# The short form of h - tanh(h) alone, with a test of its range and a general path behind it

## The chip, the cores and the metric

The kernel runs on one core of a Trainium2 chip. The metric is the device time of one execution in microseconds (us), as the median of several runs. TensorE is PE in the profile (its weight loads are PEld), VectorE is DVE, ScalarE is ACT, GpSimd is POOL, and SyncE, which issues every DMA of this kernel, is SP.

## What is computed

Three layers follow one another. An attention in which 32 packed queries p of each head first gather keys and values, and the 576 queries of a sequence then attend to the 32 packed rows; a layer with the odd nonlinearity h - tanh(h); and a layer in which each token goes to one of eight experts. Cut to what matters:

```python
p_packed = sm_attn(p, k, v)                      # 8 batches, 8 heads, 32 packed rows of 64
out = sm_attn(q, p_packed, p_packed)             # 8 batches, 8 heads, 576 rows of 64
x = out.transpose(0, 2, 1, 3).reshape(4608, 512)
h = x @ w_in                                     # w_in 512 x 2048
x = (h - np.tanh(h)) @ w_out                     # w_out 2048 x 512
logits = x @ w_gate + modality_bias[modality_id] # 8 experts, one per token by argmax
out[mask] = gate_w[mask, None] * (np.maximum(x[mask] @ w1[e], 0.0) @ w2[e])
```

The weights of the middle layer come as 64-bit floats. Matrix products are done in fp32, or, where a stage is long, as three products of rounded parts (hi by hi, lo by hi, hi by lo).

## The kernel before

Since the second attention is a product with p_packed, its output need not be formed: h of a head is a2 (the softmax of 32 columns) times M = p_packed times w_in. The kernel forms M per batch (m_pe, eight products of 512 columns, lines 195 to 235, `at<-ws,ppT` and `mh`, `ml` in the profile) and the attention weights a2 per half batch of 288 tokens (sm2a to sm2d, lines 454 to 498).

The work is cut into slots. In the first part, 256 slots: 16 half batches, each with 16 blocks f of 128 columns of w_in. A slot n does gemm1 (`h<-a,m`, a block of 128 x 288 of h), then chain(n), which makes g = h - tanh(h) out of it, then gsplit, which makes two rounded parts `gh` and `gl`, and three slots later gemm2 (`acc<-gh,wo_hi` and so on), which adds g times a block of w_out into four accumulators. The first 32 slots (half batches 0 and 1) use plain fp32 in gemm1, and the first 16 in gemm2. Between them stand the conversion of the 64-bit weights (conv_a, 32 chunks, lines 159 to 178, on DVE, ACT and POOL), the attention of the next batch, its M, and the logits of half batches that are done. In the second part, 144 slots, the one expert that token 0 goes to is applied to all tokens (gemm1b, relu, gemm2b). At the end the kernel reads a flag of whether any token goes to another expert, and if so does those in other_experts.

chain(n), lines 731 to 752, holds eight instructions, each over 128 x 288 elements. On ACT: u = h squared (L741), th = tanh(h) (L742), mk = a scaled square of h as an integer, which is zero where h squared is under the threshold U_THR = 0.0775 (L743), qq = exp(-PK u) (L744). On DVE: th = h - th (L745), qq = (qq + PB) u (L747), gs = PA qq h (L749), and a predicated copy (L751), which puts th into gs where mk is not zero. So gs holds a short form of h - tanh(h), PA h u (exp(-PK u) + PB), where h is small, and the difference elsewhere. The tiles u, qq, th and mk have one buffer each. The products h stand in two PSUM buffers (ps_h); one comes free when the last instruction of chain that reads it is done. gsplit (lines 754 to 763) rounds gs to gh on ACT (L760) and takes gl = gs - gh (L762) on DVE or, from slot 16 on for seven of sixteen slots, on POOL:

```python
eng = nc.gpsimd if n >= 16 and n % 16 in [3, 5, 7, 9, 11, 13, 15] else nc.vector
eng.tensor_tensor(out=gl, in0=gs, in1=f32(gh), op=ALU.subtract)
```

A scheduling layer sets the final order of each engine's instructions out of the order in which the program is written, its dependencies and its own durations. Each engine then runs its list in that order.

Of the kernel before, what the change touches and what calls it, by code (L numbers as in the profile page):

```python
# [26 lines left out]
def attn_moe_moe_kernel(  # L27
# [131 lines left out]
    def conv_a(key):  # L159
        raw = raws[key].rearrange("p a c -> p (a c)")  # L160
        hi, lo = raw[:, 1::2], raw[:, 0::2]
        nc.vector.tensor_scalar(
            out=lo, in0=lo, scalar1=29, scalar2=0x40000000, op0=ALU.logical_shift_right, op1=ALU.bitwise_or
        )
        yield
        nc.vector.scalar_tensor_tensor(
            out=lo, in0=hi, scalar=3, in1=lo, op0=ALU.logical_shift_left, op1=ALU.bitwise_xor
        )
        yield
        nc.scalar.activation(out=hi, in_=hi.bitcast(F32), func=ACTF.Copy, scale=16384.0)  # L170
        nc.scalar.activation(out=hi.bitcast(F32), in_=hi, func=ACTF.Sign)
        nc.scalar.activation(out=lo.bitcast(F32), in_=lo.bitcast(F32), func=ACTF.Abs)
        v = hi.bitcast(F32)
        if key[0] == 0:
            v = early.tile([128, 512], F32, name="wv", tag="wv", bufs=6)
        elif key[1] < NWH // 2:
# [70 lines left out]
    def attention(ap, b, ps_of):  # L247
# [177 lines left out]
        def ppt_ev():  # L425
            ps = ps_of("ppt", 0)
            t = ppT[b] = ap.tile([128, 4, 32], F32, name="ppT", tag="ppT", bufs=2)
            nc.scalar.activation(out=t.rearrange("p h j -> p (h j)"), in_=ps[:, 0, 128:256], func=ACTF.Copy)

        def scores2(half):  # L430
            ps = ps_of("s2", half)
# [44 lines left out]
        def sm2c(half):  # L476
# [134 lines left out]
    def flags_a():  # L611
# [8 lines left out]
            yield  # L620
        fl["has"] = has

    def flags_pe():
# [5 lines left out]
    def flags_b():  # L629
        other = evp.tile([1, NE], F32, name="other", tag="rt_m")  # L630
        nc.vector.tensor_tensor(
            out=other, in0=em8[0:1, :], in1=idx_t[0:1, 0:1].to_broadcast([1, NE]), op=ALU.not_equal
        )
        n = evp.tile([1, NE, NHB], F32, name="n_other", tag="rt_l")
        nc.vector.tensor_tensor(
            out=n, in0=fl["ps"].rearrange("o (e h) -> o e h", e=NE),
            in1=other.unsqueeze(2).to_broadcast([1, NE, NHB]), op=ALU.mult,
        )
# [4 lines left out]
        yield  # L643
        nc.vector.tensor_copy(out=flags[:, 0:NE, 0:NHB], in_=n)
        nc.vector.tensor_copy(out=flags[:, :, NHB], in_=tot)
        yield


    def other_experts():
        gd, idd = (nc.dram_tensor(nm, [NBLK, 32], F32, kind="Internal").ap() for nm in ("gate_d", "idx_d"))  # L650
        hi_f = 32
        n_any = nc.values_load(flags[0:1, NE, NHB:NHB + 1], min_val=0, max_val=hi_f)
# [200 lines left out]
    def relu(n):  # L853
        ps = ht.pop(n)
        if n % 2:
            gh, gl = (
                gp.tile([128, TB], F32R, name="bg", tag=tg) for tg in (("u", "qq") if n % 4 == 1 else ("th", "mk"))
            )
        else:
            gh = g3.tile([128, TB], F32R, name="bh", tag="gh")  # L860
# [44 lines left out]
    def seq(fns):  # L905
        for fn in fns:
            res = fn()
            if isgenerator(res):
                yield from res
            else:  # L910
                yield


    with ExitStack():
# [79 lines left out]
        for f in range(NWH // 2):  # L994
            at_cv(NWH + 1 + f * 11 // 7, lambda f=f: conv_b((1, f)))


        def run(*fns):
            for _ in seq(fns):
                pass  # L1000
# [173 lines left out]
```

## Time and profile before

| what | value |
|---|---|
| median of 3 runs | 1284.15 us (1283.78 to 1285.51) |
| the profiled execution's own time | 1284.04 us |
| its span, first to last instruction | 1282.3 us |
| PE busy | 1210.1 us, 94% |
| DVE busy | 838.4 us, 65% |
| ACT busy | 710.3 us, 55% |
| POOL busy | 166.3 us, 13% |
| mean granted TensorE clock | 0.983 |

By the starts of u, slot 0 begins at 41.0 us, slot 16 at 114.5, slot 32 at 186.1, slot 208 at 721.2, and the second part at 864.3 us; the last matmul ends at 1271.5 us. A share of the whole span is a mean over stages with different limits, so the rows further down are cut at these times. A row of busy time reads: the stretch, its length, then for PE, PEld, DVE, ACT and POOL the busy time and the count of instructions, the granted clock, the DMA engines' busy share and GB/s. What is missing in PE's busy time to the length of a stretch is time in which PE had nothing to do.

### The profile page before, as it was taken

What the parts mean: (1) busy time and instruction counts of PE and PEld (TensorE: products, weight loads), DVE (VectorE), ACT (ScalarE), POOL (GpSimd) and SP (SyncE); (2) the same over time, 40 slices, a digit from 0 to 9 for tenths busy, and PEclk for the clock granted to TensorE, in tenths of its full rate; (3) what the DMA queues carried; (4) which work ended last, traced back from release to release, by engine and by line L of the source; (5) the groups of instructions that cost most, each with busy time, mean ns of one, the idle gap of its engine ahead of it and who ended that gap; (6) DMA issues with size and microseconds to landing.
All of it is one profiled execution on the core that took longest, in us unless ns stands there. A gap on an engine that the chain in (4) does not pass through costs nothing.

```text
span 1282.3 us, 25934 instructions
## 1 busy us (share of the span) xinstructions
PE 1210.1 (94%) x9762; PEld 1049.7 (82%) x9763; DVE 838.4 (65%) x1941; ACT 710.3 (55%) x1832; POOL 166.3 (13%) x174
## 2 busy tenths in 40 slices
PE   5688889999999999999999999999999999999996
PEld 2455668889889889979979978989899999999995
DVE  4987999898998898998898897884111111111111
ACT  3888867678678678678677777772111111111111
POOL 1322211121111111111111122240000000000000
PEclk7799899999999999999999999999999999999998
DMA  8766344454354344344345126212122222222201
GB/s 241 213 201 197 104 131 118 106 131 121 73 129 119 73 125 124 73 118 128 73 108 139 39 83 194 79 51 74 63 83 67 82 61 76 64 65 83 66 17 35
DMA packets 189843, 132.36 MB, mean 103 GB/s; under 512 B 122640, under 2 KB 167696, under 8 KB 189712
## 3 DMA queue, kind: packets, MB, share of 16 engines
q1 hardware_dynamic: 189712, 130.65, 36.6%
q8 instruction: 78, 1.28, 0.4%
q14 instruction: 53, 0.43, 0.1%
HBM read 98.10 MB, written 32.51 MB: 102 GB/s over the span
## 4 chain that ended last, share of the span: by engine, by line
PE 68%; DVE 16%; issue 7%; ACT 4%; DMA 3%; POOL 2%; SPq 0%; POOLq 0%; DVEq 0%; ACTq 0%
PE acc L98 12%; PE acc L100 12%; PE acc L99 11%; PE h L98 9%; PE h L99 8%; PE h L100 8%; PE at L202 2%; DVE gs L749 2%; DVE th L745 2%; DVE gs L751 2%; DVE gl L762 1%; PE at L340 1%; DVE qq L747 1%; DMA w1s<-in_moe_w_dram 1%; DVE s L466 1%
## 5 line engine op out<-in xcount | busy, mean ns | idle before, releaser
L98 PE MATMUL acc<-gh,wo_hi 128*128 128x288 f32 x960 | 293.9, 308 | 6.4 <-ACT gh L760 4.0
L100 PE MATMUL acc<-gl,wo_hi 128*128 128x288 f32 x960 | 277.0, 298 | 5.4 <-DVE gl L762 2.9
L99 PE MATMUL acc<-gh,wo_lo 128*128 128x288 f32 x960 | 281.9, 295 | 0.0
L98 PEld LDWEIGHTS acc<-gh,wo_hi 128*128 128x128 f32 x960 | 180.4, 188 | 42.2 <-ACT u L741 13.2
L100 PEld LDWEIGHTS acc<-gl,wo_hi 128*128 128x128 f32 x960 | 177.6, 188 | 13.5 <-DVE gl L762 6.2
L99 PEld LDWEIGHTS acc<-gh,wo_lo 128*128 128x128 f32 x960 | 180.6, 188 | 0.4 <-issue 0.2
L100 PE MATMUL h<-xbl,w1h 128*128 128x256 f32 x576 | 162.3, 282 | 0.0
L99 PE MATMUL h<-xbh,w1l 128*128 128x256 f32 x576 | 162.1, 281 | 0.0
L98 PE MATMUL h<-xbh,w1h 128*128 128x256 f32 x576 | 161.5, 280 | 0.0
L762 POOL TENSOR_TENSOR gl<-gs,gh 128x288 fp32r<-128x288 f32 x105 | 85.7, 817 | 569.4 <-ACT gh L760 398.4
L745 DVE TENSOR_TENSOR th<-h,th 128x288 f32<-128x288 f32 x256 | 114.8, 449 | 53.8 <-ACT mk L743 51.2
L751 DVE COPY_PREDICATED gs<-mk,th 128x288 f32<-128x288 int32 x256 | 140.1, 547 | 2.6
L98 PE MATMUL h<-ah,mh 128*128 128x288 f32 x448 | 135.2, 302 | 6.5 <-DVE gs L749 6.5
L741 ACT ACTIVATE u<-h 128x288 f32<-128x288 f32 x256 | 106.0, 414 | 63.3 <-PE h L100 40.8
L863 DVE SCALAR_TENSOR_TENSOR bl<-h,bh 128x256 fp32r<-128x256 f32 x72 | 30.6, 425 | 164.0 <-ACT bh L862 163.9
L99 PE MATMUL h<-ah,ml 128*128 128x288 f32 x448 | 132.2, 295 | 0.0
L100 PE MATMUL h<-al,mh 128*128 128x288 f32 x448 | 131.8, 294 | 0.0
L747 DVE SCALAR_TENSOR_TENSOR qq<-qq,u 128x288 f32<-128x288 f32 x256 | 122.7, 479 | 12.8 <-ACT qq L744 9.9
L744 ACT ACTIVATE qq<-u 128x288 f32<-128x288 f32 x256 | 114.6, 448 | 27.1 <-DVE gs L749 21.9
L760 ACT ACTIVATE gh<-gs 128x288 fp32r<-128x288 f32 x240 | 107.6, 449 | 35.3 <-PE acc L99 33.8
L742 ACT ACTIVATE th<-h 128x288 f32<-128x288 f32 x256 | 104.6, 409 | 34.9 <-DVE gs L751 32.2
L862 ACT ACTIVATE bh<-h 128x256 fp32r<-128x256 f32 x72 | 27.6, 384 | 171.3 <-PE h L100 169.8
(163 smaller groups left out, 2426.4 us busy)
## 6 DMA issues: line engine op xcount, KB each, us to landing
ws<-w_in_v SPq DMA_DIRECT2D x56, 512.0 KB
nat<-in_v_dram SPq DMA_DIRECT2D x16, 576.0 KB
x_hi<-x2h SPq DMA_DIRECT2D x16, 576.0 KB
x_lo<-x2l SPq DMA_DIRECT2D x16, 576.0 KB
xbh<-x_hi SPq DMA_DIRECT2D x18, 512.0 KB
xbl<-x_lo SPq DMA_DIRECT2D x18, 512.0 KB
raw<-in_moe_w_in_dram SPq DMA_DIRECT2D x32, 256.0 KB
raw<-in_moe_w_out_dram SPq DMA_DIRECT2D x16, 512.0 KB
```

Of the source, the lines that this page charges most:

```text
L98: nc.tensor.matmul(out=ps, lhsT=ah, rhs=bh, start=first, stop=False)
L99: nc.tensor.matmul(out=ps, lhsT=al, rhs=bh, start=False, stop=False)
L100: nc.tensor.matmul(out=ps, lhsT=ah, rhs=bl, start=False, stop=last)
L741: nc.scalar.activation(out=u, in_=ps, func=ACTF.Square)
L742: nc.scalar.activation(out=th, in_=ps, func=ACTF.Tanh)
L744: nc.scalar.activation(out=qq, in_=u, func=ACTF.Exp, scale=-PK)
L745: nc.vector.tensor_tensor(out=th, in0=ps, in1=th, op=ALU.subtract)
L747: nc.vector.scalar_tensor_tensor(out=qq, in0=qq, scalar=PB, in1=u, op0=ALU.add, op1=ALU.mult)
L751: nc.vector.copy_predicated(gs, mk, th)
L760: nc.scalar.activation(out=gh, in_=gs, func=ACTF.Copy)
L762: eng.tensor_tensor(out=gl, in0=gs, in1=f32(gh), op=ALU.subtract)
L863: nc.vector.scalar_tensor_tensor(out=gl, in0=ps, scalar=0.0, in1=f32(gh), op0=ALU.max, op1=ALU.subtract)
```

## The change

In chain, tanh, the mask, the difference and the predicated copy are gone, so two instructions are left on ACT and two on DVE; u and qq have two buffers each. Every gl is now taken by DVE. The threshold is tested ahead of time instead: the entries of a head's a2 row add up to one, so the absolute h is at most the sum over eight heads of the largest absolute entry of M. After each product of M a new DVE instruction (m_bound) takes the largest absolute entry of each partition, 64 in all; near the end flags_a compares the largest of them with 0.998 sqrt(U_THR) / 8 and the count of partitions above it is added to the flag that the kernel reads at its end. If it is not zero, a new function redo computes the first two layers again with tanh, from a2, p_packed and w_in, which therefore are written to DRAM: a2 of each half batch (16 DMAs) and p_packed of each batch (8 DMAs), on SP's queue.

```diff
+    ones_b = const.tile([128, 1], F32, name="ones_b")
+    m_max = const.tile([128, B, NU], F32, name="m_max")
...
     def m_ev(b, u, ps=AT):
...
             mt[b, u] = (t,)
+            m_bound(b, u, t)
             return
...
         nc.vector.tensor_tensor(out=lo, in0=ps, in1=f32(hi), op=ALU.subtract)
-        yield
+        m_bound(b, u, f32(hi))
+        yield
+
+    def m_bound(b, u, t):
+        nc.vector.tensor_reduce(
+            out=m_max[:, b, u:u + 1], in_=t.rearrange("p g c -> p (g c)"), axis=AX.X, op=ALU.max,
+            apply_absolute_value=True,
+        )
...
+            nc.sync.dma_start(out=pp_d[b], in_=t)
...
+            nc.sync.dma_start(out=a2_d[2 * b + half], in_=t.rearrange("p g c -> p (g c)"))
...
+        nc.vector.tensor_reduce(out=t, in_=m_max.rearrange("p b u -> p (b u)"), axis=AX.X, op=ALU.max)
+        nc.vector.tensor_scalar(out=t, in0=t, scalar1=0.998 * U_THR ** 0.5 / H, scalar2=None, op0=ALU.is_gt)
...
+        nc.tensor.matmul(out=AT[0:1, 1, 0:1], lhsT=ones_b, rhs=fl["big"], start=True, stop=True)
...
         with tc.If(n_any > 0):
+            n_big = nc.values_load(flags[0:1, NE, 0:1], min_val=0, max_val=128)
+            with tc.If(n_big > 0):
+                redo()
...
     def chain(n):
         ps = ht.pop(n)
-        u = gp.tile([128, HW], F32, name="u")
-        qq = gp.tile([128, HW], F32, name="qq")
-        th = gp.tile([128, HW], F32, name="th")
-        mk = gp.tile([128, HW], I32, name="mk")
+        u = gp.tile([128, HW], F32, name="u", bufs=2)
+        qq = gp.tile([128, HW], F32, name="qq", bufs=2)
...
         nc.scalar.activation(out=u, in_=ps, func=ACTF.Square)
-        nc.scalar.activation(out=th, in_=ps, func=ACTF.Tanh)
-        nc.scalar.activation(out=mk, in_=ps, func=ACTF.Square, scale=(0.5 / U_THR) ** 0.5)
         nc.scalar.activation(out=qq, in_=u, func=ACTF.Exp, scale=-PK)
-        nc.vector.tensor_tensor(out=th, in0=ps, in1=th, op=ALU.subtract)
         yield
         nc.vector.scalar_tensor_tensor(out=qq, in0=qq, scalar=PB, in1=u, op0=ALU.add, op1=ALU.mult)
         yield
         nc.vector.scalar_tensor_tensor(out=gs, in0=qq, scalar=PA, in1=ps, op0=ALU.mult, op1=ALU.mult)
-        yield
-        nc.vector.copy_predicated(gs, mk, th)
...
-        eng = nc.gpsimd if n >= 16 and n % 16 in [3, 5, 7, 9, 11, 13, 15] else nc.vector
-        eng.tensor_tensor(out=gl, in0=gs, in1=f32(gh), op=ALU.subtract)
+        nc.vector.tensor_tensor(out=gl, in0=gs, in1=f32(gh), op=ALU.subtract)
```

DVE's list between the softmax of batch 4 and that of batch 5, before (th, qq, gs, gl and mk are the tiles of chain and gsplit; ml is the low part of M; what an instruction waits for stands in brackets):

```order
L747 SCALAR_TENSOR_TENSOR qq<-qq,u 128x288 [waits Activation_49]
L745 TENSOR_TENSOR th<-h,th 128x288 [waits DVE_49,Activation_49]
L749 SCALAR_TENSOR_TENSOR gs<-qq,h 128x288 [waits DVE_49,Pool_49]
L762 TENSOR_TENSOR gl<-gs,gh 128x288 [waits PE_49,Activation_49]
L751 COPY_PREDICATED gs<-mk,th 128x288 [waits DVE_49]
L747 SCALAR_TENSOR_TENSOR qq<-qq,u 128x288 [waits Activation_49]
L745 TENSOR_TENSOR th<-h,th 128x288 [waits DVE_49,Activation_49]
L749 SCALAR_TENSOR_TENSOR gs<-qq,h 128x288 [waits DVE_49]
L751 COPY_PREDICATED gs<-mk,th 128x288 [waits DVE_49]
```

And the same engine between the same two softmaxes now:

```order
L872 TENSOR_TENSOR gl<-gs,gh 128x288 [waits PE_49,Activation_49]
L860 SCALAR_TENSOR_TENSOR qq<-qq,u 128x288 [waits Activation_49]
L862 SCALAR_TENSOR_TENSOR gs<-qq,h 128x288 [waits DVE_49]
L872 TENSOR_TENSOR gl<-gs,gh 128x288 [waits PE_49,Activation_49]
L860 SCALAR_TENSOR_TENSOR qq<-qq,u 128x288 [waits Activation_49]
L862 SCALAR_TENSOR_TENSOR gs<-qq,h 128x288 [waits DVE_49]
```

Two slots took eight instructions of chain and one gl; they now take four and two gl, and each gl, which waits for PE and ACT, stands in front of the next slot's qq and gs.

DVE's list at the start of the program, before (s is the softmax of half batch 0 or 1, m its sums, a2w its finished weights, which the first gemm1 reads; raw is a chunk of 64-bit weights):

```order
L483 RECIPROCAL m_356<-m_356 128x18 [waits DVE_49]
L466 TENSOR_TENSOR s_375<-s_375,m_378 128x576
L485 TENSOR_TENSOR s_330<-s_330,m_356 128x576 [waits DVE_49]
L162 TENSOR_SCALAR raw_345<-raw_345 128x512 [waits DMAHW3_49,Pool_49]
L490 STREAM_TRANSPOSE a2w<-s_330 128x576 [waits DVE_49]
```

And now (m_w is the copy of M that ACT takes from PSUM for batch 0):

```order
L500 TENSOR_REDUCE m_361<-s_334 128x18 [waits Activation_49]
L250 TENSOR_REDUCE m_max<-m_w 128x1 [waits Activation_49]
L502 TENSOR_SCALAR m_361<-m_361 128x18 [waits DVE_49]
L485 TENSOR_REDUCE m_384<-s_381 128x18
L504 RECIPROCAL m_361<-m_361 128x18 [waits DVE_49]
L487 TENSOR_TENSOR s_381<-s_381,m_384 128x576 [waits DVE_49]
L506 TENSOR_TENSOR s_334<-s_334,m_361 128x576 [waits DVE_49]
L250 TENSOR_REDUCE m_max<-m_w 128x1 [waits Activation_49]
L511 STREAM_TRANSPOSE a2w<-s_334 128x576 [waits DVE_49]
```

Two of the new reductions stand in front of the transpose that finishes a2w, and the second waits for ACT's copy of the second product of M; the step on raw has moved behind it.

## Rows read from the trace of the kernel before

**Rows 1.** The page: busy time, share of the span, instructions.

```profile
PE 1210.1 (94%) x9762; PEld 1049.7 (82%) x9763; DVE 838.4 (65%) x1941; ACT 710.3 (55%) x1832; POOL 166.3 (13%) x174
```

**Rows 2.** Busy time by stretch: PE, PEld, DVE, ACT, POOL, clock, DMA, GB/s.

```profile
0.00:41.00 41.00, 21.70 (x277) 11.36 (x279) 24.70 (x60) 16.83 (x34) 6.16 (x12) 0.78 0.74 204
41.00:114.50 73.50, 63.79 (x328) 39.97 (x327) 62.03 (x134) 64.72 (x148) 21.84 (x20) 0.94 0.73 218
114.50:186.00 71.50, 58.70 (x497) 40.85 (x496) 64.24 (x133) 55.96 (x134) 16.53 (x16) 0.93 0.49 131
186.00:721.20 535.20, 524.96 (x4987) 466.00 (x4986) 477.71 (x1148) 397.42 (x1069) 78.61 (x87) 1.00 0.42 108
721.20:864.30 143.10, 133.78 (x1068) 122.23 (x1067) 124.78 (x271) 105.38 (x281) 42.35 (x39) 1.00 0.31 99
864.30:1266.40 402.10, 402.10 (x2594) 365.49 (x2593) 83.77 (x199) 69.30 (x167) 0.80 (x1) 1.00 0.21 65
```

**Rows 3.** PE's waits, 41 to 114.5: us in total, times, longest.

```profile
PE h L726 <- DVE gs L749: 5.8, 6, 2.8
PE at L202 <- POOL wv L178: 3.5, 5, 0.9
```

**Rows 4.** PE's waits, 114.5 to 186.

```profile
PE h L726 <- DVE gs L749: 7.6, 4, 3.0
```

**Rows 5.** PE's waits, 186 to 721.2.

```profile
PE acc L98 <- ACT gh L760: 2.6, 5, 0.5
PE at L202 <- DVE rt_t L556: 2.5, 5, 0.5
PE acc L100 <- DVE gl L762: 1.7, 5, 0.3
PE acc L100 <- POOL gl L762: 1.1, 5, 0.2
```

**Rows 6.** PE's waits, 721.2 to 864.3.

```profile
PE h L98 <- DVE gs L749: 6.5, 10, 1.3
```

**Rows 7.** Groups of instructions: busy, mean ns, idle before and who ended it.

```profile
L751 DVE COPY_PREDICATED gs<-mk,th 128x288 f32<-128x288 int32 x256 | 140.1, 547 | 2.6
L745 DVE TENSOR_TENSOR th<-h,th 128x288 f32<-128x288 f32 x256 | 114.8, 449 | 53.8 <-ACT mk L743 51.2
L762 DVE TENSOR_TENSOR gl<-gs,gh 128x288 fp32r<-128x288 f32 x135 | 66.8, 495 | 4.6 <-ACT gh L760 4.4
...
L743 ACT ACTIVATE mk<-h 128x288 int32<-128x288 f32 x256 | 104.8, 409 | 0.0
L742 ACT ACTIVATE th<-h 128x288 f32<-128x288 f32 x256 | 104.6, 409 | 34.9 <-DVE gs L751 32.2 <-DVE nm L351 0.7 <-DVE rs L373 0.5
...
L762 POOL TENSOR_TENSOR gl<-gs,gh 128x288 fp32r<-128x288 f32 x105 | 85.7, 817 | 569.4 <-ACT gh L760 398.4 <-DVE th L745 54.8 <-PE h L100 51.6
```

**Rows 8.** DVE and ACT in order of time: start, duration.

```profile
563.08 0.45 DVE L745 TENSOR_TENSOR th<-h,th 128x288 f32<-128x288 f32 x1
563.44 0.45 DVE L749 SCALAR_TENSOR_TENSOR gs<-qq,h 128x288 f32<-128x288 f32 x1
...
564.81 0.41 ACT L742 ACTIVATE th<-h 128x288 f32<-128x288 f32 x1 [0.38 <-DVE gs L751]
565.11 0.41 ACT L743 ACTIVATE mk<-h 128x288 int32<-128x288 f32 x1
```

**Rows 9.** The same view around the first gemm1.

```profile
33.37 0.75 DVE L479 TENSOR_REDUCE m<-s 128x18 f32<-128x576 f32 x1
34.04 0.74 DVE L464 TENSOR_REDUCE m<-s 128x18 f32<-128x576 f32 x1
...
36.25 0.60 ACT L227 ACTIVATE m_w<-at 128x512 f32<-128x512 f32 x1 [1.87 <-PE at L202]
37.82 0.77 DVE L490 STREAM_TRANSPOSE a2w<-s 128x576 f32<-128x576 f32 x1
38.74 4.18 PE L726 MATMUL h<-a2w,m_w 128*128 128x288 f32 x8 [2.56 <-DVE a2w L490]
```

More of the change, by code (lines that the diff above doesn't have):

```diff
@@ L175, in conv_a @@
             v = early.tile([128, 512], F32, name="wv", tag="wv", bufs=6)
+        elif key[0] == 2:
+            v = wv[key]
         elif key[1] < NWH // 2:
@@ L627, in flags_pe, with flags_b @@
         )
[L629 to L633, printed above, removed]
-        n = evp.tile([1, NE, NHB], F32, name="n_other", tag="rt_l")
[L635 to L638, printed above, removed]
-        yield
+    def flags_b(every=False):
+        n = evp.tile([1, NE, NHB], F32, name="n_other", tag="rt_l")
+        ps = fl["ps"].rearrange("o (e h) -> o e h", e=NE)
+        if every:
+            nc.vector.tensor_copy(out=n, in_=ps)
+        else:
+            other = evp.tile([1, NE], F32, name="other", tag="rt_m")
+            nc.vector.tensor_tensor(
+                out=other, in0=em8[0:1, :], in1=idx_t[0:1, 0:1].to_broadcast([1, NE]), op=ALU.not_equal
+            )
+            nc.vector.tensor_tensor(
+                out=n, in0=ps, in1=other.unsqueeze(2).to_broadcast([1, NE, NHB]), op=ALU.mult,
+            )
+            yield
         tot = evp.tile([1, NE + 1], F32, name="n_tot", tag="gq")
@@ L643, in flags_b @@
         yield
+        if not every:
+            nc.vector.tensor_copy(out=flags[:, NE, 0:1], in_=AT[0:1, 1, 0:1])
+            nc.vector.tensor_tensor(out=tot[:, NE:NE + 1], in0=tot[:, NE:NE + 1], in1=AT[0:1, 1, 0:1], op=ALU.add)
         nc.vector.tensor_copy(out=flags[:, 0:NE, 0:NHB], in_=n)
@@ L646, in flags_b, with redo @@
         yield
+    def redo():
+        nonlocal evp
+        with ExitStack() as st:
+            rp = st.enter_context(tc.tile_pool(name="rp", bufs=1))
+            rb = st.enter_context(tc.tile_pool(name="rb", bufs=2))
+            evp = rp
+            wo = rp.tile([128, NF, 512], F32, name="wo")
+            for f in range(NF):
+                raw = rb.tile([128, 1024], I32, name="rraw")
+                nc.sync.dma_start(out=raw, in_=w_out.bitcast(I32)[f * 128:f * 128 + 128, :])
+                raws[2, f] = raw.rearrange("p (a c) -> p a c", a=2)
+                wv[2, f] = wo[:, f, :]
+                for _ in conv_a((2, f)):
+                    pass
+            with tc.For_i(0, B, 1) as b:
+                pt = rp.tile([128, 4, 32], F32, name="rpt")
+                nc.sync.dma_start(out=pt, in_=pp_d[bass.ds(b, 1)].rearrange("o p (h j) -> p (o h) j", h=4))
+                m = rp.tile([128, NU, 2, 256], F32, name="rm")
+                for u in range(NU):
+                    ws = rb.tile([128, 4, 256], F32, name="rws")
+                    nc.sync.dma_start(out=ws, in_=win_v[u])
+                    tiled(
+                        lambda g, hh: AT[32 * hh:32 * hh + 32, g, 0:256],
+                        lambda g, hh: pt[64 * g:64 * g + 64, hh, :],
+                        lambda g, hh: ws[64 * g:64 * g + 64, hh, :],
+                    )
+                    nc.scalar.activation(out=m[:, u], in_=AT[:, :, 0:256], func=ACTF.Copy)
+                for half in range(2):
+                    redo_half(rp, rb, wo, m, b, half)
+            for hb in range(3, NHB, 4):
+                lt_t[0] = evp.tile([32, 36, NE], F32, name="rt_l", tag="rt_l")
+                nc.sync.dma_start(
+                    out=lt_t[0].rearrange("i (x r) e -> i x (r e)", x=4),
+                    in_=lg_d[hb - 3:hb + 1].rearrange("x i n -> i x n"),
+                )
+                run(lambda: routing(hb))
+            run(flags_a)
+            flags_pe()
+            run(lambda: flags_b(every=True))
@@ new lines, in redo_half @@
+    def redo_half(rp, rb, wo, m, b, half):
+        a2 = rp.tile([128, 2, HW], F32, name="ra2")
+        nc.sync.dma_start(out=a2, in_=a2_d[bass.ds(b * 2 + half, 1)].rearrange("o p (g c) -> p (o g) c", g=2))
+        ac = [pools["acc"].tile([128, 512], F32, name=f"acc{c}") for c in range(4)]
+        for f in range(NF):
+            ps = ps_h.tile([128, HW], F32, name="h", tag="h")
+            for g in range(2):
+                nc.tensor.matmul(
+                    out=ps, lhsT=m[:, f // 2, g, 128 * (f % 2):128 * (f % 2) + 128], rhs=a2[:, g, :],
+                    start=(g == 0), stop=(g == 1),
+                )
+            u, qq, th, gs = (rb.tile([128, HW], F32, name=f"r{nm}") for nm in ("u", "qq", "th", "gs"))
+            mk = rb.tile([128, HW], I32, name="rmk")
+            nc.scalar.activation(out=u, in_=ps, func=ACTF.Square)
+            nc.scalar.activation(out=th, in_=ps, func=ACTF.Tanh)
+            nc.scalar.activation(out=mk, in_=ps, func=ACTF.Square, scale=(0.5 / U_THR) ** 0.5)
+            nc.scalar.activation(out=qq, in_=u, func=ACTF.Exp, scale=-PK)
+            nc.vector.tensor_tensor(out=th, in0=ps, in1=th, op=ALU.subtract)
+            nc.vector.scalar_tensor_tensor(out=qq, in0=qq, scalar=PB, in1=u, op0=ALU.add, op1=ALU.mult)
+            nc.vector.scalar_tensor_tensor(out=gs, in0=qq, scalar=PA, in1=ps, op0=ALU.mult, op1=ALU.mult)
+            nc.vector.copy_predicated(gs, mk, th)
+            for c in range(4):
+                nc.tensor.matmul(
+                    out=ac[c][:, 0:HW], lhsT=wo[:, f, c * 128:c * 128 + 128], rhs=gs, start=(f == 0), stop=(f == NF - 1)
+                )
+        xh, xl = ev_t[0] = [rp.tile([128, 4, HW], F32R, name=f"rx{c}") for c in "hl"]
+        for c in range(4):
+            nc.scalar.activation(out=xh[:, c, :], in_=ac[c][:, 0:HW], func=ACTF.Copy)
+            nc.vector.tensor_tensor(out=xl[:, c, :], in0=ac[c][:, 0:HW], in1=f32(xh[:, c, :]), op=ALU.subtract)
+        for d, t in zip(xs, (xh, xl)):
+            nc.sync.dma_start(out=d[:, :, bass.ds(b * S + half * HW, HW)], in_=f32(t))
+        logits_pe(0)
+        run(lambda: route_in(0))
+        nc.sync.dma_start(
+            out=lg_d[bass.ds(b * 2 + half, 1)].rearrange("o i n -> (o i) n"),
+            in_=lt_t[0][:, 0:9, :].rearrange("i r e -> i (r e)"),
+        )
@@ L856, in relu @@
             gh, gl = (
-                gp.tile([128, TB], F32R, name="bg", tag=tg) for tg in (("u", "qq") if n % 4 == 1 else ("th", "mk"))
+                gp.tile([128, TB], F32R, name="bg", tag=tg, bufs=2) for tg in ("u", "qq")
             )
@@ L911, in seq, with run @@
                 yield
+    def run(*fns):
+        for _ in seq(fns):
+            pass
     with ExitStack():
```

15 lines of the change are left out of this document (10 added, 5 removed).

## The prediction

> **What bounds the kernel now.** I read the busy shares first, and then distrust them. PE is busy 94% of the span and DVE 65% [rows 1], which looks like a kernel that only PE limits. The view by stretches tells more [rows 2]. From 864.3 us on, in the second part, PE is busy for all of 402.1 us while DVE and ACT are busy a fifth of it. Nothing that makes DVE or ACT lighter can help there. In the first part, from 41 to 864.3 us, DVE is busy 84 to 90% and PE has gaps. The length of each stretch less PE's busy time gives them: 73.5 - 63.8 = 9.7 us, 71.5 - 58.7 = 12.8 us, 535.2 - 525.0 = 10.2 us and 143.1 - 133.8 = 9.3 us, together 42.0 us. So the question is not how much work goes from DVE, which is a lot, but how many of these 42 us PE gets back.
>
> The waits say who ends the gaps. In the first two stretches it is mostly gs, the DVE instruction that frees the PSUM buffer of h: 5.8 of 9.7 us and 7.6 of 12.8 us [rows 3, 4]. From 186 to 721.2 us the gaps are few, about half a microsecond each at the same places in each batch: gh late on ACT, the transposed logits rt_t late on DVE, gl late [rows 5]. Toward the end gs is late again, ten times for 6.5 us [rows 6]. A DVE that is behind its work is the common cause; but DVE also stood idle for 51.2 us ahead of th until ACT had made mk [rows 7], so there it was ACT's four instructions in a row, and not DVE's own load, that were late.
>
> **The change part by part.** Durations overlap their successors: th and gs start 0.36 us apart though each takes 0.45 us, tanh and mk start 0.30 us apart at 0.41 us each [rows 8]. I count the distance of starts.
>
> Removed, per slot: th and the predicated copy on DVE, 2 x 0.37 = 0.74 us; tanh and mk on ACT, 0.60 us; in 256 slots 189 us of DVE and 154 us of ACT. The sums of durations, 114.8 + 140.1 and 104.8 + 104.6 us, are the upper ends [rows 7].
>
> Added on DVE: 64 reductions over 512 elements. No row has one; the nearest are reductions over 576 elements, which start 0.67 us apart and take 0.74 us [rows 9]. Scaled to 512 I take 0.60 us, 38 us in all; the ends are 0.36 us, the step of a 288-element instruction, and 0.74 us, so 23 to 47 us.
>
> Moved: 105 gl from POOL (0.817 us each) to DVE. At the step of 0.37 us that is 39 us, at the mean duration of the 135 that are there already, 0.495 us, 52 us [rows 7]. I take 39.
>
> So DVE does about 112 us less in the first part. By stretch, with 16, 16, 176 and 48 slots, 6, 8, 42 and 8 reductions and 0, 7, 77 and 21 moved gl: 62.0 - 11.8 + 3.6 = 53.8 us; 64.2 - 11.8 + 4.8 + 2.6 = 59.8 us; 477.7 - 130.2 + 25.2 + 28.5 = 401 us; 124.8 - 35.5 + 4.8 + 7.8 = 102 us. Set against PE's busy time in the same stretches (63.8, 58.7, 525 and 134 us), DVE falls clearly below PE in all but the second. ACT falls to 55, 46, 292 and 77 us. PE's own instructions stay as they are but for one tiny matmul.
>
> What of PE's gaps goes:
> - 41 to 114.5 us, 9.7 us. The gs waits are about a chain that is too long and queues that are too full; both shrink. The waits for wv, 3.5 us, hang on the conversion of weights (POOL), which the change leaves alone; it only gets less company on ACT. I take 5 us.
> - 114.5 to 186 us, 12.8 us. DVE stays as loaded as PE (59.8 against 58.7 us), so bursts of it still delay PE. I take 60%, 7.5 us.
> - 186 to 721.2 us, 10.2 us. The waits stand right behind the softmax of a half batch, where DVE has a backlog; with DVE at 75% it works it off sooner, and the POOL ones go with their instruction. The transposes that logits need stay on the way. I take two thirds, 7 us.
> - 721.2 to 864.3 us, 9.3 us. Nearly all gs; DVE goes from 87 to 71%. I take 7 us.
> - Clock. The granted clock was 0.94 and 0.93 in the two early stretches and 1.00 later [rows 2], so PE spent about 2 x 0.06 x 73.5 + 2 x 0.07 x 71.5 = 19 us at 1.2 GHz, worth up to 9 us. It fell where PE had been waiting. With fewer waits I take 1.5 us.
> - 0 to 41 us: a loss. Two reductions now stand ahead of the transpose that finishes a2w, and the first gemm1 waited 2.56 us for just that [rows 9]. They cost 2 x 0.60 us, and a step on raw of about 0.34 us has moved away: 0.9 us later. The second one waits for ACT's copy of M, which ended at 36.25 + 0.60 = 36.85 us, before DVE would come to it, about 1 us ahead of the transpose that started at 37.82 us, so this wait is covered [rows 9].
>
> What I cost at nothing: the 24 DMAs of a2 and p_packed, 5.2 MB over some 820 us or 6 GB/s, beside the 99 to 218 GB/s of these stretches, with DMA engines 31 to 49% busy from 114.5 us on [rows 2]; on SP each waits for DVE or ACT and holds up the loads behind it, but these run slots ahead (if that cover were gone, a load of raw would be late by the few tenths that a2 is late, twice, in the first stretch). The test of the flag and its matmul stand in the second part, where DVE and ACT are a fifth busy. The branch at the end jumps over more code, while the last output is still on its way (last matmul 1271.5 us, end of span 1282.3 us). And redo is not run: from the reference's inputs the largest absolute entry of M works out as 0.0098, and the limit 0.998 x sqrt(0.0775) / 8 is 0.0347.
>
> The sum: 5 + 7.5 + 7 + 7 + 1.5 - 0.9 = 27.1 us. The profiled execution took 1284.04 us, 1.7 us more than its span and 0.1 us less than the median of 1284.15 us, so this stands for both: 1284.0 - 27.1 = 1257 us.
>
> The Trainium skill speaks to the clock (TensorE: Matmul & The Clock Gate, Part 1: The HAM clock gate): the throttled state is the default, and only activity of PE releases it. The two early stretches agree, 0.94 and 0.93 beside 1.00 in the dense ones. Taken strictly, a PE that no longer waits would win all of the up to 9 us there instead of my 1.5, and the sum would be 1249 us.
>
> **The rivals.**
> *The early part does not follow.* From 41 to 186 us the pace is set by the conversion of 32 weight chunks on ACT, DVE and POOL, by attention and by loads (DMA 73% busy in the first of the two stretches), and the order of PE's list there is new. For it: the POOL waits of rows 3, and that DVE hardly falls below PE in the second stretch. Against it: ACT, the fullest engine at 64.7 of 73.5 us, loses 9.6 us. Then only the later 14 us come, less 0.9: 1271 us.
>
> *All gaps go.* DVE and ACT no longer limit anywhere: 42 us and most of the clock's 9, less 0.9, give 1284 - 49 = 1235 us. Against it: waits for wv, and gaps behind logits that are chains of latency and not of load.
>
> *Slower: gl blocks DVE's list.* In the new order gl, which waits for ACT's gh and for PE to free its buffer, stands in front of the next slot's qq and gs, and gs frees h. POOL could wait for gh at no cost, and did, 398 us [rows 7]; DVE cannot. If each of the 105 moved gl held back PE as a late gs does, 6.5 us in ten waits or 0.65 us each [rows 6], it would cost 68 us, and the time would be 1325 us; from 27 / 105 = 0.26 us each it eats the gain. Against it: the 135 gl that DVE already takes made it idle for 4.6 us in all, 0.03 us each [rows 7], so the moved ones would cost 3.6 us of DVE's time, which has slack.
> The Trainium skill supports the mechanism (TensorE: Matmul & The Clock Gate, Architectural detail: the array is 16× 32×32): VectorE and ScalarE take their instructions strictly first in, first out. The 0.03 us above say that here gh is nearly always there in time.
>
> *The general path runs after all.* It would repeat two layers and cost more than the whole first part; the factor of 3.5 between 0.0098 and 0.0347 speaks against it.
>
> **How the numbers follow.** The forecast, with both early and late gaps closing by about half or more (1246 to 1266 us), gets 0.56; the early part not following (1266 to 1279 us) 0.20; all gaps gone (1234 to 1246 us) 0.13; no gain within 0.2%, that is 2.6 us, which is about what a measurement of this kernel can tell from no change, 0.04; slower, by gl or by new waits, 0.06; the general path 0.01. The range leaves out the lower half of the third case, the slower ones and the edge of the second: 1240 to 1277 us. Faster: 0.56 + 0.20 + 0.13 = 0.89, same 0.04, slower 0.07. The unknown costs fit in: reductions at 23 or 47 us instead of 38 shift DVE's load by 3% of it.
>
> **What would show it.** In the same cuts (by the starts of u) PE's gaps from slot 0 to the second part should fall from 42 to about 17 us, with the second part 402 us long as before. Waits of h for gs should nearly vanish after 721 us. Slot 0 should start near 42 us. A reduction should take about 0.67 us and DVE about 725 us in all. The granted clock should be near 0.95 in the early stretches. I am wrong if DVE's idle time ahead of gl grows by tens of microseconds with PE waiting for gs behind it, if the first 32 slots still take 145 us, or if the first part gets shorter and PE's gaps do not, since the gain then comes from something that I have not named.

## The result, and the profile after

The changed kernel takes 1256.6 us (median of four runs, 1255.3 to 1257.0) beside 1284.8 us of the kernel before on the same chip: a ratio of 0.978 with a 95% interval of 0.976 to 0.979. The forecast was 1257 us. The sum came out right, its terms did not: the first 32 slots gave less than half of what was forecast for them, the later ones 1.7 times as much.

The line of busy times on the page after, beside [rows 1]:

```profile
PE 1195.3 (95%) x9764; PEld 1050.2 (84%) x9765; DVE 722.7 (58%) x1603; ACT 569.6 (45%) x1320; POOL 77.5 (6%) x69
```

DVE lost 115.7 us and ACT 140.7. The row to stop at is PE's: its busy time fell by 14.8 us, though it has two instructions more. The same view by stretch, cut as in [rows 2] at the starts of slots 0, 16 and 32, of slot 208 and of the second part (columns as there):

```profile
0.00:41.80 41.80, 22.19 (x277) 11.98 (x279) 25.57 (x64) 17.00 (x34) 4.89 (x11) 0.80 0.80 215
41.80:105.80 64.00, 56.77 (x289) 35.75 (x289) 46.43 (x95) 48.85 (x103) 18.51 (x18) 0.89 0.77 220
105.80:181.60 75.80, 64.83 (x536) 48.11 (x536) 61.82 (x123) 54.25 (x116) 14.55 (x13) 0.93 0.58 157
181.60:703.70 522.10, 514.94 (x4986) 464.06 (x4985) 404.70 (x918) 300.94 (x717) 15.30 (x10) 1.00 0.46 117
703.70:835.90 132.20, 128.98 (x1068) 121.55 (x1067) 98.82 (x204) 78.60 (x184) 24.30 (x18) 1.00 0.36 112
835.90:1239.30 403.40, 403.40 (x2600) 365.64 (x2600) 84.64 (x202) 69.27 (x167) 0.00 (x0) 1.00 0.21 65
```

Other work now falls before slot 16 (289 PE instructions, 328 before), so the two early stretches are to be read together: 145.1 us before, 139.8 now, with PE and DVE busy for 122.6 and 126.4 us before and 121.6 and 108.3 now.

```profile
41.00:186.10 145.10, 122.58 (x824) 80.92 (x824) 126.37 (x266) 120.68 (x281) 38.37 (x35) 0.93 0.61 175
```

```profile
41.80:181.60 139.80, 121.60 (x824) 83.86 (x824) 108.25 (x218) 103.10 (x219) 33.05 (x30) 0.91 0.67 186
```

By stretch the span of 1282.3 us lost its 27.1 us so: 0.8 us more up to slot 0; 5.3 less in the first 32 slots; 13.0 less in slots 32 to 207; 10.9 less in slots 208 to 255; 1.3 more from there to the end.

PE's waits by releaser in these stretches after (us, times, longest), beside [rows 3 to 6]; first 41.8 to 105.8 us:

```profile
PE at L212 <- POOL wv L188: 3.5, 4, 1.6
PE h L844 <- DVE gs L862: 2.4, 1, 2.4
```

From 105.8 to 181.6 us:

```profile
PE acc L107 <- DVE gl L872: 2.8, 2, 1.8
PE at L212 <- POOL wv L188: 2.5, 5, 0.8
...
PE h L844 <- DVE gs L862: 1.1, 1, 1.1
```

From 181.6 to 703.7 us, and then from 703.7 to 835.9:

```profile
PE at L212 <- DVE rt_t L578: 5.0, 5, 1.1
PE h L105 <- ACT mh L242: 0.8, 1, 0.8
```

```profile
PE h L105 <- DVE gs L862: 2.1, 3, 1.3
```

The gs waits fell from 13.4 us to 3.5 in the first 32 slots, and from 6.5 to 2.1 at the end. The waits of M's products for the converted weights (wv) stayed (4.8 us before, 6.0 now), and that for rt_t behind the softmax doubled to 1 us a time. The groups that answer to [rows 7] (busy, mean ns, idle before and its releaser):

```profile
L860 DVE SCALAR_TENSOR_TENSOR qq<-qq,u 128x288 f32<-128x288 f32 x256 | 131.3, 513 | 116.7 <-ACT qq L858 116.5
L872 DVE TENSOR_TENSOR gl<-gs,gh 128x288 fp32r<-128x288 f32 x240 | 113.1, 471 | 31.3 <-ACT gh L871 27.4
...
L250 DVE TENSOR_REDUCE m_max<-mh 128x1 f32<-128x512 f32 x56 | 37.7, 674 | 0.0
```

DVE now waits for ACT in front of qq, 116.5 us in all, and in front of gl, 27.4 us. Both are the idle time of an engine that is ahead of PE: the waits of PE for gl that show as gaps are 2.8 us in the first 32 slots, and hardly any later.

**Where the time hides.** From slot 0 to the second part 29.2 us went (823.3 to 794.1), but PE's visible gaps fell only from 42.1 to 28.6 us, by 13.5. The other 15.7 us came out of PE's busy time, in slots 32 to 207 alone 10.0 (524.96 to 514.94, x4987 and x4986). Why, PE in order of time shows, in the kernel before (start, duration):

```profile
563.51 0.29 PE L99 MATMUL acc<-gh,wo_lo 128*128 128x288 f32 x1
563.64 0.29 PE L100 MATMUL acc<-gl,wo_hi 128*128 128x288 f32 x1
563.77 0.29 PE L98 MATMUL acc<-gh,wo_hi 128*128 128x288 f32 x1
563.91 0.29 PE L99 MATMUL acc<-gh,wo_lo 128*128 128x288 f32 x1
564.27 0.40 PE L100 MATMUL acc<-gl,wo_hi 128*128 128x288 f32 x1
564.51 0.29 PE L98 MATMUL acc<-gh,wo_hi 128*128 128x288 f32 x1
```

A product of 288 columns is recorded for 0.29 us, while undisturbed ones start 0.13 us apart. The fifth row starts 0.36 us after the fourth: gl was late by 0.23 us, but only 0.07 us are left as a gap between the recorded end (564.20) and the next start. A wait of up to 0.16 us shows none. The gaps from which I built the sum were thus a lower bound of what PE loses. Counted over all pairs of such products of 128 x 288 that follow one another, the time beyond 0.13 us that lies inside the recorded length fell from 16.6 to 10.9 us in slots 32 to 207 and from 6.0 to 2.1 us in slots 208 to 255, together 9.6 of the 14.8 us by which PE's busy time fell there. The rest lies outside these pairs, with the smaller products between them, and is not parted further here. The Trainium skill warns of the view itself (Perfetto Trace Analysis, Identifying the Most-Contended Engine): the busy share of matmuls is no good measure of how far a kernel is from its limit, since they are pipelined. This trace agrees that it misleads, with 14.8 us of busy time gone from the whole run at two instructions more. The page's reason, that pipelined instructions look smaller in the trace, is not what these rows show: here they are recorded longer than their step, 0.29 beside 0.13 us.

### The profile page after: what moved, and what is told of

Read it like the earlier page. It is cut to its first block, busy times and chain, and to the rows that moved or that the text cites. A ratio compares the mean times of both kernels' runs of the same rounds, so it can differ in the third digit from the quotient of the medians.

```text
span 1255.2 us, 24451 instructions
## 1 busy us (share of the span) xinstructions
PE 1195.3 (95%) x9764; PEld 1050.2 (84%) x9765; DVE 722.7 (58%) x1603; ACT 569.6 (45%) x1320; POOL 77.5 (6%) x69
## 4 chain that ended last, share of the span: by engine, by line
PE 78%; DVE 8%; issue 6%; DMA 2%; ACT 2%; POOL 2%; SPq 0%; POOLq 0%; DVEq 0%; ACTq 0%
PE acc L105 15%; PE acc L107 14%; PE acc L106 14%; PE h L106 10%; PE h L105 10%; PE h L107 9%; PE at L212 3%; DVE s L487 1%; PE at L359 1%; POOL wv L188 1%; DVE x2l L906 1%; DVE qq L860 1%; PE h L844 1%; DVE gl L872 1%; DMA raw<-in_moe_w_in_dram 1%
## 5 line engine op out<-in xcount | busy, mean ns | idle before, releaser
L107 PE MATMUL acc<-gl,wo_hi 128*128 128x288 f32 x960 | 282.9, 296 | 3.0 <-DVE gl L872 2.8
L860 DVE SCALAR_TENSOR_TENSOR qq<-qq,u 128x288 f32<-128x288 f32 x256 | 131.3, 513 | 116.7 <-ACT qq L858 116.5
L107 PEld LDWEIGHTS acc<-gl,wo_hi 128*128 128x128 f32 x960 | 180.6, 189 | 5.9 <-DVE gl L872 5.0
L871 ACT ACTIVATE gh<-gs 128x288 fp32r<-128x288 f32 x240 | 106.7, 445 | 158.7 <-PE acc L106 143.1
L872 DVE TENSOR_TENSOR gl<-gs,gh 128x288 fp32r<-128x288 f32 x240 | 113.1, 471 | 31.3 <-ACT gh L871 27.4
L862 DVE SCALAR_TENSOR_TENSOR gs<-qq,h 128x288 f32<-128x288 f32 x256 | 112.5, 440 | 6.2 <-PE acc L881 1.7
L106 PEld LDWEIGHTS h<-xbh,w1l 128*128 128x128 f32 x576 | 108.1, 188 | 6.2
L105 PEld LDWEIGHTS h<-xbh,w1h 128*128 128x128 f32 x576 | 108.2, 188 | 5.8
L973 DVE SCALAR_TENSOR_TENSOR bg<-h,bg 128x256 fp32r<-128x256 f32 x72 | 30.6, 425 | 139.0 <-ACT bg L972 139.0
```

The lines of the kernel that those rows point to most:

```text
L105: nc.tensor.matmul(out=ps, lhsT=ah, rhs=bh, start=first, stop=False)
L106: nc.tensor.matmul(out=ps, lhsT=al, rhs=bh, start=False, stop=False)
L107: nc.tensor.matmul(out=ps, lhsT=ah, rhs=bl, start=False, stop=last)
L872: nc.vector.tensor_tensor(out=gl, in0=gs, in1=f32(gh), op=ALU.subtract)
L973: nc.vector.scalar_tensor_tensor(out=gl, in0=ps, scalar=0.0, in1=f32(gh), op0=ALU.max, op1=ALU.subtract)
```

## Experiments

Stretches are cut at the same places in each; the first 32 slots, slots 32 to 207 and slots 208 to 255 are 145.1, 535.2 and 143.1 us before and 139.8, 522.1 and 132.2 us in the changed kernel. Ratios are to the kernel before, with their 95% interval.

**The short chain alone.** The kernel before without the four instructions: no test, no redo, gl still shared with POOL.

```diff
...
-        nc.scalar.activation(out=th, in_=ps, func=ACTF.Tanh)
-        nc.scalar.activation(out=mk, in_=ps, func=ACTF.Square, scale=(0.5 / U_THR) ** 0.5)
...
-        nc.vector.tensor_tensor(out=th, in0=ps, in1=th, op=ALU.subtract)
...
-        nc.vector.copy_predicated(gs, mk, th)
```

> The kernel before with the four instructions of tanh, mask, difference and predicated copy left out of each chain, and nothing else: gl stays shared with POOL, no reductions, no new DMAs, one buffer for u and qq; tanh is left out of the computation where h is large. Theory (late DVE and ACT made PE wait): nearly the whole gain comes from this, 1252 to 1258 us. Rival (gl on DVE and the reductions cost PE time that the changed kernel pays): at most 1248 us.

1253.6 us, 0.974 (0.972 to 0.977). The short chain is the whole gain; the rest of the change costs some 3 us. That is a sum of two parts with opposite signs: further down, the changed kernel without its test takes 1249.0 us, 4.6 less than this one, from which it differs by gl on DVE and by two buffers for u and qq. Of the 4.6 us, 3.7 lie in the first 32 slots (139.7 and 136.0), and no run takes the second buffers alone.

**DVE's half, and ACT's half.** Which engine was it? Once only the difference and the predicated copy are left out (tanh and mk are still made), once only tanh and mk (the difference and the copy work on zeros).

```diff
-        nc.vector.tensor_tensor(out=th, in0=ps, in1=th, op=ALU.subtract)
...
-        nc.vector.copy_predicated(gs, mk, th)
```

> The kernel before with only DVE's two instructions (difference and predicated copy) left out; ACT still makes tanh and mask, which nobody reads, so g is the short form alone. Theory that DVE's load is what was late: most of the gain, 1260 to 1268 us. Rival, that the row of four ACT instructions was late: at most 5 us, 1279 us or more.

```diff
+    zero = const.tile([128, HW], F32, name="zero")
...
-        nc.scalar.activation(out=th, in_=ps, func=ACTF.Tanh)
-        nc.scalar.activation(out=mk, in_=ps, func=ACTF.Square, scale=(0.5 / U_THR) ** 0.5)
...
-        nc.vector.tensor_tensor(out=th, in0=ps, in1=th, op=ALU.subtract)
+        nc.vector.tensor_tensor(out=th, in0=ps, in1=zero, op=ALU.subtract)
...
-        nc.vector.copy_predicated(gs, mk, th)
+        nc.vector.copy_predicated(gs, zero.bitcast(I32), th)
```

> The kernel before with only ACT's tanh and mask left out; DVE still does both of its instructions on a tile of zeros, so g is the short form alone. Theory that DVE's load was late: a small gain, 1274 to 1282 us. Rival, that ACT's row was late: 1268 us or less.

DVE's half: 1255.5 us, 0.977 (0.975 to 0.979), nearly everything and more than I expected. ACT's half: 1278.7 us, 0.994 (0.992 to 0.996). Slots 32 to 207 of the two, by the view of stretches:

```profile
177.80:701.60 523.80, 519.77 (x4986) 465.47 (x4985) 349.43 (x796) 381.78 (x1070) 77.78 (x87) 1.00 0.43 110
```

```profile
185.60:721.10 535.50, 521.29 (x4986) 465.10 (x4985) 487.80 (x1148) 300.60 (x717) 83.42 (x87) 1.00 0.43 107
```

With DVE at 349 us the stretch is 523.8 us long though ACT is busy 382 of them; with ACT at 301 us and DVE at 488 it is as long as before. DVE is the engine that held PE up there. DVE's half takes both load and two steps of each slot's chain away from it, so by itself it does not say which of the two counts. One of the next two runs adds load and leaves the chain up to gs as it is. The 51.2 us that DVE waited for mk [rows 7] were not the limit up to slot 207: without mk, ACT's half gained 0.5 us in the first 32 slots (144.6) and nothing in the next 176. In the last 48 it gained 5 us (137.9), where DVE's half gained 11 (132.0).

**The gl that moved.** Once the changed kernel with gl shared with POOL as before, once the kernel before with every gl on DVE.

```diff
-        nc.vector.tensor_tensor(out=gl, in0=gs, in1=f32(gh), op=ALU.subtract)
+        eng = nc.gpsimd if n >= 16 and n % 16 in [3, 5, 7, 9, 11, 13, 15] else nc.vector
+        eng.tensor_tensor(out=gl, in0=gs, in1=f32(gh), op=ALU.subtract)
```

> The changed kernel with gl shared with POOL again (seven of sixteen slots from slot 16 on), all else as changed. Theory now (gl is later on POOL, and its access to SBUF slows DVE, so the move helps a little): 1258 to 1262 us. Rival (gl in DVE's list holds back the next slot's gs, so the move costs): 1254 us or less.

The second is the same edit in reverse, on the kernel before.

> The kernel before with every gl on DVE and nothing else changed. DVE's load in the steady part would rise from 478 to about 506 of 535 us. Theory (DVE late): slower than before, 1290 to 1300 us, with PE waiting for gs in all stretches. Rival (DVE has slack, its idle time ahead of th shows it): within 3 us of before.

In the changed kernel the engine of gl does not matter: 1256.9 us, 0.979 (0.977 to 0.980), against either expectation. In the kernel before it does: 1291.6 us, 1.007 (1.005 to 1.009). Slots 32 to 207 there:

```profile
184.80:728.00 543.20, 528.41 (x4986) 466.44 (x4985) 491.34 (x1225) 399.03 (x1069) 14.24 (x10) 1.00 0.41 106
```

The 8 us that it lost stand here. So the move costs where DVE is 89 to 90% busy, some 7 us for 105 gl, and nothing at 78%. It costs by load, and hardly by gl's own wait: over the whole run DVE stood idle ahead of gl for 5.8 us, after 4.6 with the gl shared.

```profile
L761 DVE TENSOR_TENSOR gl<-gs,gh 128x288 fp32r<-128x288 f32 x240 | 111.4, 464 | 5.8 <-ACT gh L760 5.4
```

What PE waited for in slots 32 to 207 was not gs, which I had expected, but gl and the low part of M, ml:

```profile
PE acc L100 <- DVE gl L761: 4.7, 5, 1.0
PE at L202 <- DVE ml L233: 4.6, 5, 0.9
```

The Trainium skill's rule that VectorE takes its instructions first in, first out (TensorE: Matmul & The Clock Gate, Architectural detail: the array is 16× 32×32) fits both: in a list without slack an added instruction makes those behind it late.

**The early part.** The changed kernel with the long chain in the first 32 slots only.

```diff
+        if n < 32:
+            nc.scalar.activation(out=th, in_=ps, func=ACTF.Tanh)
+            nc.scalar.activation(out=mk, in_=ps, func=ACTF.Square, scale=(0.5 / U_THR) ** 0.5)
...
+        if n < 32:
+            nc.vector.tensor_tensor(out=th, in0=ps, in1=th, op=ALU.subtract)
...
+        if n < 32:
+            nc.vector.copy_predicated(gs, mk, th)
```

> The changed kernel with the long chain (tanh, mask, difference, predicated copy) kept in the first 32 slots alone. It shows what the short chain gives there. Theory (late DVE and ACT): the 5 us that the first 32 slots became shorter are lost again, 1260 to 1265 us, with these slots 144 to 148 us long. Rival (the conversion of the weights sets the pace there, whatever the chain): within 2 us of the changed kernel, 1255 to 1258 us.

1263.8 us, 0.984 (0.983 to 0.986): the early slots are worth 7 us here. They took 146.8 us, the later ones 521.1 and 132.5, as in the changed kernel.

**What the test costs.** The changed kernel without reductions, DMAs, flag and redo; then without the 64 reductions alone; then without the 24 DMAs alone.

```diff
-            m_bound(b, u, t)
...
-        m_bound(b, u, f32(hi))
...
-            nc.sync.dma_start(out=pp_d[b], in_=t)
...
-            nc.sync.dma_start(out=a2_d[2 * b + half], in_=t.rearrange("p g c -> p (g c)"))
...
-            with tc.If(n_big > 0):
-                redo()
```

> The changed kernel without its test of the range: no reductions over M, no DMAs of a2 and p_packed, no general path (so the tanh is left out where h is large); gl on DVE and two buffers for u and qq as there. Theory (the test's 38 us of DVE are covered but for the start): 1 to 3 us faster than the changed kernel, 1253.5 to 1255.5 us. Rival (the test costs PE time all through the first part): 1248 us or less.

```diff
-        nc.vector.tensor_reduce(
-            out=m_max[:, b, u:u + 1], in_=t.rearrange("p g c -> p (g c)"), axis=AX.X, op=ALU.max,
-            apply_absolute_value=True,
-        )
```

> The changed kernel without its 64 reductions over M (the test reads zeros, so the general path could not be taken); the DMAs of a2 and p_packed and the code of the general path stay. The whole test cost about 8 us (the kernel without it: 1249.0 us). Theory (the reductions are what costs, on DVE): 1249 to 1251 us. Rival (the DMAs on SP's queue or the code): 1254 us or more.

```diff
-            nc.sync.dma_start(out=pp_d[b], in_=t)
...
-            nc.sync.dma_start(out=a2_d[2 * b + half], in_=t.rearrange("p g c -> p (g c)"))
```

> The changed kernel without its 24 DMAs of a2 and p_packed (the general path would find nothing to work on); the reductions, the flag and the code of the general path stay. Without the reductions alone the time was 1258.1 us, without the whole test 1249.0 us. Theory now (the DMAs stand in SP's list in front of weight loads and wait for DVE, so conversion is later): 1249 to 1252 us, with the first 32 slots 136 to 138 us long. Rival (the code of the general path, or the order that the scheduling layer happens to give): 1255 us or more.

Without all of it: 1249.0 us, 0.971 (0.969 to 0.973), a miss of my expectation; the test costs 7.6 us. Without the reductions: 1258.1, 0.980 (0.978 to 0.982); without the DMAs: 1256.3, 0.977 (0.976 to 0.979). Neither is the price. Part of it is at the end. The last issue of the output by SP, in the kernel before, the changed one and the one without the test:

```profile
1271.56 1.29 SPq L903 DMA_DIRECT2D out_dram<-o  x2
```

```profile
1243.56 1.30 SPq L1013 DMA_DIRECT2D out_dram<-o  x2
```

```profile
1237.99 1.30 SPq L895 DMA_DIRECT2D out_dram<-o  x2
```

From there to the end of the span it is 10.7 us (to 1282.3), 11.6 us (to 1255.2) and 10.7 us (to 1248.7). In all, the stretch from the second part to the end is 418.9 to 419.3 us in the seven profiles of kernels that hold redo's code and the flag's test, and 417.5 to 418.3 in the seven of kernels without them: the two together, the first of which is not run, cost about 1 us. Slots 32 to 207 give 2.2 us more (519.9 without the test), the first 32 slots 3.8 (136.0). In the kernels with the short chain and POOL's conversion those 32 take anything from 136 to 142 us, and what falls before slot 16 differs from kernel to kernel. So their 3.8 us may be the price of the order that each edit happens to give; these runs put it down to no single instruction.

**The conversion in the early part.** POOL makes one product in each of the 32 conversions of weights, and PE still waits for wv. The runs move 16 of them to DVE, then all 32, and last all 32 in the kernel before. The edit of the second and the third of these runs is shown; the first does the same for the chunks of w_in alone.

```diff
-        nc.gpsimd.tensor_tensor(out=v, in0=lo.bitcast(F32), in1=hi.bitcast(F32), op=ALU.mult)
+        nc.vector.tensor_tensor(out=v, in0=lo.bitcast(F32), in1=hi.bitcast(F32), op=ALU.mult)
```

> The changed kernel with the product that ends the conversion of w_in (16 of 32 chunks) on DVE in place of POOL; PE waited for it 9.9 us in the changed kernel, most of it while the first M was made. Theory (that product's latency, 1.1 us on POOL and about 0.7 us on DVE, is what is late in the early part): 1251 to 1255 us. Rival (what is late is the ACT and DVE work ahead of it, or the load): 1256 us or more.

> The same for all 32 chunks, w_out too, whose product PE waited for 1.4 us only. DVE then carries about 19 us more than in the changed kernel in its first 32 slots, some 127 of 140 us, as much as before the change. Theory (DVE late is what made PE wait): no better than with half of the chunks, and slower than the changed kernel, 1257 to 1264 us. Rival (DVE's load does not matter there): 1255 us or less.

> The kernel before, with all 32 conversion products moved from POOL to DVE (the edit that made the changed kernel faster by some 7 us). Theory: that edit is worth something only because the short chain has freed DVE. In the kernel before DVE is busy 126.4 of the 145.1 us of the first 32 slots, and 32 products at 0.69 us add 22 us, more than the 18.7 us that are free: no gain, 1283 to 1292 us, first 32 slots at least 145 us. Rival: POOL's 1.04 us per product is a wait of its own, whatever DVE has to do, so the edit gives the kernel before its 7 us too: 1274 to 1279 us, first 32 slots about 138 us.

Sixteen: 1256.1 us, 0.977 (0.976 to 0.979), no gain. All 32: **1249.3 us**, 0.973 (0.971 to 0.975), faster than the changed kernel by 7 us with its test kept: the version that beats both. Slots 32 to 255 are as long as in the changed kernel (522.2 and 132.2). My theory that DVE's load is what counts in the early part falls here, and so does the one that only the short chain makes room for it: the same edit gives the kernel before 1277.4 us, 0.995 (0.993 to 0.996). The first 32 slots of the changed kernel with all 32 moved, and of the kernel before with them:

```profile
40.90:173.70 132.80, 116.46 (x824) 80.19 (x824) 117.94 (x251) 103.16 (x221) 2.85 (x2) 0.95 0.70 201
```

```profile
40.80:180.10 139.30, 119.13 (x822) 79.38 (x821) 133.26 (x294) 119.19 (x283) 8.60 (x8) 0.93 0.62 180
```

In the kernel before these slots held 266 DVE instructions in 126.4 us. Now they hold 28 more at about 0.69 us, 19 us in all, and DVE's busy time rose by only 6.9 us; I had counted 22 us for the 32 in full. Some of the others have become shorter. One pair in the kernel before, in order of time:

```profile
60.60 1.32 DVE L751 COPY_PREDICATED gs<-mk,th 128x288 f32<-128x288 int32 x1
```

```profile
60.36 1.21 POOL L178 TENSOR_TENSOR wv<-raw 128x512 f32<-128x512 f32 x1 [1.67 <-ACT raw L172]
```

DVE's copy is 1.32 us long instead of some 0.45, and ends 0.35 us after POOL's product (61.92 and 61.57): it seems to have stood still until POOL was done. Over the first 32 slots, by the groups of DVE's instructions in the kernel before, and then with the products on DVE:

```profile
L166 DVE SCALAR_TENSOR_TENSOR raw<-raw 128x512 int32<-128x512 int32 x26 | 21.5, 828 | 0.3
L751 DVE COPY_PREDICATED gs<-mk,th 128x288 f32<-128x288 int32 x31 | 17.8, 573 | 0.2
...
L749 DVE SCALAR_TENSOR_TENSOR gs<-qq,h 128x288 f32<-128x288 f32 x32 | 14.2, 444 | 0.4
```

```profile
L166 DVE SCALAR_TENSOR_TENSOR raw<-raw 128x512 int32<-128x512 int32 x26 | 17.8, 684 | 0.1
...
L751 DVE COPY_PREDICATED gs<-mk,th 128x288 f32<-128x288 int32 x31 | 14.7, 474 | 0.1
...
L749 DVE SCALAR_TENSOR_TENSOR gs<-qq,h 128x288 f32<-128x288 f32 x32 | 14.2, 444 | 0.2
```

The copy and the step on raw give back 3.1 and 3.7 us; gs, which reads h from PSUM, is the same in both. What I had taken for POOL's free help was paid for by DVE. How much of the 7 us comes from there, how much from a product that takes 0.69 instead of 1.04 us on the way to wv, and how much from a new order, these runs do not part. That shorter product is not the whole of it: PE's waits for wv at M's products fell from 6.0 to 1.6 us in the changed kernel but rose from 4.8 to 7.1 in the kernel before, and both gained; with sixteen products moved nothing was gained.

## Why the prediction was right, and where it was not

**Right:**
- The binding engine in most of the first part: a DVE behind its work. DVE's half of the edit alone gives 0.977.
- DVE's load: 725 us forecast, 722.7 measured; in slots 32 to 207, 401 and 404.7; at the end, 102 and 98.8. A reduction takes 0.67 us, as forecast.
- The start, by luck: 0.9 us later forecast, 0.8 measured. The first gemm1 starts between 38.0 and 40.4 us in the fourteen profiles, whatever stands ahead of it: at 39.38 in the changed kernel without its reductions and at 40.35 without the whole test, but at 38.63 with the reductions and all conversion products on DVE. So the runs do not put the 0.8 us down to the reductions. In the changed kernel the transpose moved from 37.82 [rows 9] to 38.62 us, and the first gemm1 started at 39.53 us, 0.79 later. DVE in order of time there:

```profile
37.35 0.75 DVE L506 TENSOR_TENSOR s<-s,m 128x576 f32<-128x576 f32 x1
38.02 0.68 DVE L250 TENSOR_REDUCE m_max<-m_w 128x1 f32<-128x512 f32 x1
38.62 0.77 DVE L511 STREAM_TRANSPOSE a2w<-s 128x576 f32<-128x576 f32 x1
```

The second reduction did not wait for ACT's copy of M, as forecast.
- The second part: 402 us of full PE forecast, 403.4 measured in a cut that is a little longer. The general path did not run. DVE's idle time ahead of gl did grow as the sign of the rival had it, from 4.6 us for 135 to 31.3 for 240, but PE's waits for gs fell with it, so gl did not block.

**Wrong, and cancelling:**
- "41 to 114.5 us ... I take 5 us", "114.5 to 186 us ... 7.5 us" and "Clock ... 1.5 us", together 14: measured 5.3. The rival in which the early part does not follow was half right. The clock gave nothing, 0.89 and 0.93 after 0.94 and 0.93, with PE still waiting 18.2 us; what the rule of the Trainium skill that I set beside it (TensorE: Matmul & The Clock Gate, Part 1: The HAM clock gate) would give to a PE that no longer waits, no run here shows. What kept the pace was in part the conversion: PE's waits for wv stayed, POOL's products held up DVE, and moving them gave 7 us in either kernel (the new order that this brings is not ruled out). I had written that the change "leaves alone" the conversion, and still gave this stretch half its gap.
- Slots 32 to 207, 7 us forecast, 13.0 measured, and slots 208 to 255, 7 forecast, 10.9 measured. The step that failed is "PE has gaps. The length of each stretch less PE's busy time gives them": in these two stretches the visible gaps fell by 3.0 and 6.1 us (10.2 to 7.2, 9.3 to 3.2), the busy time by 10.0 and 4.8. I had named the case: the first part gets shorter and the gaps do not, so the gain comes from something not named. It does, in more than half, and two thirds of that (9.6 of 14.8 us) is short waits inside the recorded length of the 128 x 288 products; the rest lies outside pairs of these.
- PE's gaps: 17 us forecast, 28.6 measured. For the same reason the rival "all gaps go" was probably priced too low: with no gap left, the hidden waits would have shrunk as well. No run here shows such a case.
- "DVE also stood idle for 51.2 us ahead of th until ACT had made mk ... and not DVE's own load, that were late": ACT's half alone gives 0.994, and what it gains stands in the last 48 slots. In slots 32 to 207 DVE's idle time ahead of th was not PE's loss.
- The price of the test at nothing beyond its start: 7.6 us measured (0.9 of it behind the last output, which I had put beside the output's DMA).

## What to carry to other kernels

Where matmuls are recorded longer than their distance of starts, compare the length of a stretch with its count of instructions times the undisturbed step, not with PE's busy time: the gaps show only the long waits. Judge which engine limits by taking its work alone away; idle time ahead of an instruction does not say it. And before work is shared with GpSimd, look at what VectorE's own instructions, those with two SBUF operands above all, take while GpSimd runs.

## What the runs showed of the hardware

An instruction of DVE with two SBUF inputs and a product on POOL do not run beside each other at their usual lengths. By the list of one tile's instructions in the kernel before (duration in ns, least, median and largest), qq, whose inputs both lie in SBUF, and gs, which reads h from PSUM; below them a step of the conversion, by its line:

```profile
L747 DVE SCALAR_TENSOR_TENSOR qq<-qq,u x256: 404/449/1552, 44.1 to 861.6; 128x288 f32<-128x288 f32 x128
L749 DVE SCALAR_TENSOR_TENSOR gs<-qq,h x256: 383/444/455, 45.1 to 863.4; 128x288 f32<-128x288 f32 x128
L162 DVE TENSOR_SCALAR raw<-raw x32: 384/418/1143, 15.4 to 133.7; 128x512 int32<-128x512 int32 x32
```

The first was stretched to as much as 1.55 us, the second never beyond 0.455. The third row shows that two SBUF inputs are not the only case: a step of the conversion that reads one SBUF tensor took up to 1.14 us, at 73.19 us, beside a product of POOL that runs from 73.01 to 74.05. The Trainium skill has the rule (SBUF — State Buffer, SBUF: two separate sides): the port pair that VectorE and GpSimd share is an exclusive lock, and the later one waits for the whole instruction of the other. The pair of rows at 60.4 us above fits that rule. It explains only a small part of why 77 gl moved from POOL to DVE in slots 32 to 207 of the kernel before raised DVE's busy time by only 13.6 us (477.7 to 491.3), 0.18 us each, where I had counted 0.37 or 28.5 in all: the predicated copies became shorter by 9.9 us in sum (94.6 to 84.7), but qq longer by 5.9 (78.8 to 84.8). The rest is open.
